# One chip core, attention feeding a routed two-layer product: expert chosen from a batch's first tiles, and three interleaved chains of attention steps

## The chip, the cores and the metric

One core of one Trainium2 chip. The metric is device time in microseconds (us) of one execution of the whole kernel. Before the change it is 468.69 us, the median of 3 runs (467.3 to 468.9).

## The reference

Eight batches of 8 heads, 576 tokens and 64 dimensions go through an attention with 32 memory slots; the result is the input of a mixture of eight experts of which each token uses one.

```python
def _attn_ref(q, k, v, phi):
    a = np.exp(phi - np.max(phi, axis=2, keepdims=True))
    a = a / (np.sum(a, axis=2, keepdims=True) + 1e-09)
    k_m = np.einsum('bhsm,bhsd->bhmd', a, k)          # 32 slots per head
    v_m = np.einsum('bhsm,bhsd->bhmd', a, v)
    scores = np.matmul(q, k_m.transpose(0, 1, 3, 2)) / np.sqrt(q.shape[-1])
    attn = np.exp(scores - np.max(scores, axis=-1, keepdims=True))
    attn = attn / (np.sum(attn, axis=-1, keepdims=True) + 1e-09)
    return np.matmul(attn, v_m)

def _moe_ref(x, expert_emb, tau, w1, w2):             # x: 4608 x 512
    xn = x / (np.linalg.norm(x, axis=-1, keepdims=True) + 1e-06)
    en = expert_emb / (np.linalg.norm(expert_emb, axis=-1, keepdims=True) + 1e-06)
    logits = xn @ en.T / tau
    expert_idx = np.argmax(logits, axis=1)            # one expert per token
    probs = softmax(logits)
    gate_w = probs[np.arange(N), expert_idx]
    for e in range(8):
        m = expert_idx == e
        out[m] = gate_w[m, None] * (np.maximum(x[m] @ w1[e], 0) @ w2[e])
```

With these inputs all 576 tokens of a batch choose the same expert, so the repair loop for other experts (`rest`) has nothing to do.

## The kernel before

A batch is 576 tokens, cut into five tiles of 128 (the fifth has 64, doubled). For each batch the kernel computes the slots (`slots`, tile `acc`), turns and scales them (`block`, `flip`), multiplies them with the queries (`scores`, tiles `ts`, `tl`, copied to `sT`), and folds the values with the router's rows into `vv` (`products`). A `Tokens` object then takes the batch's tokens: `weigh` (tile `sc`, its largest subtracted, exponential into `ea`), `divide` (by its sum `z`), `turn` (transposed through `ta` into `aw`, and split by `part` into the two halves `aT` of a product in two precisions), `attend` (tile `po`: the router's logits `lg` and one-hot choices `oh`), `norm` (lengths, `ss`), `choose` (counts the choices of all five tiles on TensorE in `key`, writes the winner to `seli`, from which SyncE's queue reads which weights to load), `flags`, `root` and `gates` (some twenty small VectorE instructions and one exponential, ending in the batch's `gate`).

The expert's products of a batch are `project` (values times `w1`, tile `pg`, split into `gh` by ScalarE, L604, and `gl` by VectorE, L605), `first` (16 products `ph`, eight for each half of the tokens; each leaves by ScalarE's `hh`, L626, and then VectorE's `hl`, L627; those of the second half also by ScalarE's `h4`, L633, queued between one `hh` and the next) and `second` (tile 4 from L649, in 8 parts, then tiles 0 to 3 from L660, 32 parts). Between the parts `split_w` splits `w2` (L581 to L590). Four PSUM banks serve the products (`mm`), three the attention (`pt`), one `acc`.

The order on every engine is the order of the program. It is written out by hand up to batch 1's scores (L888 to L956). From there a planner decides: `plan` keeps a counter for each engine, each step adds a fixed price to it, and after each part of a product `run` takes the next attention steps of one single list while the step is due and neither VectorE's nor ScalarE's counter is more than `slack`, 1.8 us, ahead of TensorE's. The list (`attention`, L689) is: batch 0's late steps (flags, root, gates), batch 1's steps W, D, R, A0, N0, A1, N1, A2, C, N2, S, and then for each next batch its memory steps (E, M0, Z, late steps of the batch before, B, V, M1, B, V, T) and its token steps. `hold` stops M1, the second half of the slots, until the next batch has been projected, so that it can stand between `project` and `first`.

Around the change:

- batch 0 is attended whole (`attend` of five tiles, `choose`, L930 to L933) before batch 1's slots and scores, which end the written order;
- `run(attention)` at L956 and inside `project(0)` (L722) takes batch 0's flags, root and gates before the planner looks at anything else;
- `w2s` holds batch 1's queries until its scores are done, so `w2` of batch 0 is loaded after them (L949).

Of the kernel before, what the change touches and what calls it, by code (L numbers as in the profile page):

```python
# [30 lines left out]
CHUNKS = (((0,), (0, 1, 2, 3)), ((1,), (0, 1, 2, 3)), ((0, 1), (4,)))  # L31
HS = S // 2
OOB = 65536.0
# [16 lines left out]
class Tokens:  # L50


    def __init__(self, k, b, pt):
        self.k, self.nc, self.b, self.pt = k, k.nc, b, pt
        wk = k.wk.tile
        self.lg = wk([P, NT, E], F32, tag="lg", name=f"lg{b}")
        self.ss = wk([P, NT], F32, tag="ss", name=f"ss{b}")
        self.m = wk([P, NT], F32, tag="m", name=f"m{b}")
        self.oh = wk([P, NT, E], BF16, tag="oh", name=f"oh{b}")
        self.po = {}  # L60

    def rows(self, p):

        gs, ti = CHUNKS[p]
        x = self.k.ea[:, gs[0], :4] if p < 2 else self.k.ea[:, :, 4]
        return gs, ti, x.rearrange("p t (h m) -> p t h m", m=M)

    def weigh(self, p):
# [11 lines left out]
        k.end["sc", b, p] = d  # L80
        k.end["x", b, p] = k.plan("ACT", 0.22 + 0.1 * n, d)

    def divide(self, p):
# [7 lines left out]
        nc.vector.tensor_tensor(out=x, in0=x, in1=z.unsqueeze(3).broadcast_to(x.shape), op=ALU.mult)  # L91
        k.end["a", b, p] = k.plan("DVE", 0.6 + 0.3 * n, k.end["x", b, p])

    def turn(self, p):
# [3 lines left out]
        for l, g in enumerate(gs):  # L98
            for n, i in enumerate(ti):
                nc.tensor.transpose(t[:, l, n * P : n * P + P], k.ea[:, g, i], k.ident)  # L100
# [3 lines left out]
        n = 4 if p < 2 else 2  # L104
        k.end["aT", b, p] = k.plan("ACT", 0.2 + 0.1 * n, k.plan("PE", 0.11 * n))
        k.part(g, slice(to.start, min(to.stop, S)))

    def attend(self, *ti, pt=None):

        k, nc, b = self.k, self.nc, self.b  # L110
        for i in ti:
            self.po[i] = po = (pt or self.pt)([P, NC * (D + E)], f"po{b}_{i}")
            to = slice(T0[i], T0[i] + P)
            for g in range(NG):
                nc.tensor.matmul(po[:, 144 * g : 144 * g + P + E], lhsT=k.aw[:, g, to], rhs=k.vv[:, g], start=True, stop=True)  # L115
# [11 lines left out]
    def norm(self, *ti):  # L127
        k, nc = self.k, self.nc
        for i in ti:
            x = k.ea[:, :, i].rearrange("p g (k m) -> p g k m", k=2)  # L130
# [10 lines left out]
            k.end["po", self.b, i] = k.plan("DVE", 0.5)  # L141

    def choose(self, pt=None):

        k, nc, b = self.k, self.nc, self.b
        self.key = key = (pt or self.pt)([P, E], f"key{b}")
        for i in range(-1, NT):
            nc.tensor.matmul(
                key, lhsT=k.ones, rhs=k.eb if i < 0 else self.oh[:, i], start=i < 0, stop=i == NT - 1
            )  # L150
# [5 lines left out]
        k.plan("DVE", 0.35, k.plan("PE", 0.35))  # L156
        k.chosen.add(b)
        k.loads()

    def flags(self):  # L160

        k, nc, b, key = self.k, self.nc, self.b, self.key
        cm = k.wk.tile([P, 1], F32, tag="cm", name=f"cm{b}")
        own = k.wk.tile([P, E], F32, tag="own", name=f"own{b}")
        nc.vector.tensor_reduce(out=cm, in_=key, axis=AX.X, op=ALU.max)
        nc.vector.tensor_scalar(out=own, in0=key, scalar1=cm, scalar2=None, op0=ALU.is_equal)
        nc.vector.scalar_tensor_tensor(
            out=k.fl[:, b], in0=key, scalar=float(E), in1=own, op0=ALU.is_ge, op1=ALU.subtract
        )
        k.plan("DVE", 0.6)  # L170
# [41 lines left out]
    def steps(self):  # L212
# [4 lines left out]
        def past():  # L217

            return b - 1 < k.hidden
# [6 lines left out]
        yield "W", lambda: end["sT", b, 1] if k.late else LATE, lambda: each(self.weigh)  # L226
        for p in range(3):
            yield "D", lambda p=p: end["x", b, p], lambda p=p: self.divide(p)
        yield "R", lambda: end["a", b, 2] if past() else LATE, lambda: each(self.turn)
        yield "A0", lambda: max(end["aT", b, 0], end["aT", b, 1], end["v", b]), lambda: self.attend(0, 1)  # L230
        yield "N0", lambda: end["po", b, 1], lambda: self.norm(0, 1)
        yield "A1", lambda: end["po", b, 1], lambda: self.attend(2, 3)
        yield "N1", lambda: end["po", b, 3], lambda: self.norm(2, 3)
        yield "A2", lambda: max(end["po", b, 3], end["aT", b, 2]), lambda: self.attend(4)
# [754 lines left out]
```

## Time and profile before

| | |
|---|---|
| median of 3 runs | 468.69 us |
| profiled execution | 467.85 us, of which 466.0 us are the span shown in its trace |
| TensorE products busy | 433.3 us (93%), 3588 matmuls |
| VectorE, ScalarE, GpSimdE busy | 263.7 us (57%), 204.0 us (44%), 130.1 us (28%) |
| head, to the start of batch 0's products | 44.0 us |
| batch 0, from its products to batch 1's | 57.8 us |
| batch 1 | 53.8 us |
| batches 2 to 5, each | 52.6 us |
| batch 6, batch 7 with the end | 49.5 us, 50.5 us |

A batch is counted here from its first `pg` product to the next batch's. Busy time of TensorE is modelled, so its share alone doesn't say how dense the stream is; a batch's length against its neighbours' does.

### The profile page before, as it was taken

What the parts mean: (1) busy time and instruction counts of PE and PEld (TensorE: products, weight loads), DVE (VectorE), ACT (ScalarE), POOL (GpSimd) and SP (SyncE); (2) the same over time, 40 slices, a digit from 0 to 9 for tenths busy, and PEclk for the clock granted to TensorE, in tenths of its full rate; (3) what the DMA queues carried; (4) which work ended last, traced back from release to release, by engine and by line L of the source; (5) the groups of instructions that cost most, each with busy time, mean ns of one, the idle gap of its engine ahead of it and who ended that gap; (6) DMA issues with size and microseconds to landing.
All of it is one profiled execution on the core that took longest, in us unless ns stands there. A gap on an engine that the chain in (4) does not pass through costs nothing.

```text
span 466.0 us, 9511 instructions
## 1 busy us (share of the span) xinstructions
PE 433.3 (93%) x3588; PEld 347.6 (75%) x3588; DVE 263.7 (57%) x858; ACT 204.0 (44%) x527; POOL 130.1 (28%) x140
## 2 busy tenths in 40 slices
PE   3758699999999999999999999999999999999992
PEld 2454587868788787878788787878788787879682
DVE  5574658665677457646577357656587457555100
ACT  4334463156523564147523464147523464136310
POOL 1020122304440153304440063304440053306310
PEclk9979799999999999999999999999999999999997
DMA  8747940099315980199315980199314800183011
GB/s 298 249 166 262 334 185 23 36 339 355 133 34 197 361 291 11 46 344 359 125 34 188 371 289 11 46 337 371 119 34 176 316 2 12 47 321 148 14 46 49
DMA packets 26323, 82.48 MB, mean 177 GB/s; under 512 B 7064, under 2 KB 7064, under 8 KB 24224
## 3 DMA queue, kind: packets, MB, share of 16 engines
q1 hardware_dynamic: 23088, 72.10, 43.7%
q0 software_dynamic: 3072, 9.44, 5.6%
q8 instruction: 30, 0.49, 0.4%
q10 hardware_dynamic: 112, 0.28, 0.2%
q14 instruction: 21, 0.17, 0.1%
HBM read 66.60 MB, written 15.20 MB: 176 GB/s over the span
## 4 chain that ended last, share of the span: by engine, by line
PE 81%; issue 6%; DVE 5%; ACT 3%; DMA 2%; POOL 1%; POOLq 0%; DVEq 0%; ACTq 0%
PE py L660 34%; PE ph L623 21%; PE py L649 6%; PE acc L456 4%; PE po L115 4%; PE pg L601 2%; PE sc L73 2%; PE ts L502 2%; PE ta L100 2%; PE te L443 2%; DMA kx<-kv 1%; DMA kl<-kvt 1%; POOL wl L590 1%; DVE hl L627 1%; ACT hh L626 1%
## 5 line engine op out<-in xcount | busy, mean ns | idle before, releaser
L623 PE MATMUL ph<-aT,gh 128*128 128x288 f32 x512 | 108.9, 307 | 5.4 <-DVE gl L605 5.2
L590 POOL TENSOR_TENSOR wl<-w2s,wh 128x512 fp32r<-128x512 f32 x60 | 76.6, 1282 | 117.8 <-ACT wh L581 101.7
L660 PE MATMUL py<-wh,hh 128*128 128x512 f32 x256 | 105.8, 413 | 0.0
L660 PE MATMUL py<-wh,hl 128*128 128x512 f32 x256 | 100.4, 392 | 0.0
L660 PE MATMUL py<-wl,hh 128*128 128x512 f32 x256 | 100.0, 391 | 0.0
L623 PEld LDWEIGHTS ph<-aT,gh 128*128 128x128 f32 x512 | 83.1, 192 | 13.5 <-DVE gl L605 8.9
L627 DVE SCALAR_TENSOR_TENSOR hl<-ph,hh 128x288 fp32r<-128x288 f32 x128 | 57.6, 456 | 60.8 <-ACT hh L626 60.8
L623 PE MATMUL ph<-aT,gl 128*128 128x288 f32 x256 | 76.3, 298 | 0.0
L667 ACT ACTIVATE ys<-py,gate 128x512 f32<-128x512 f32 (+1 forms) x40 | 25.6, 641 | 90.4 <-issue 55.1
L770 POOL DMA_DIRECT2D out_dram<-ys x32 | 17.7, 552 | 155.7 <-ACT ys L667 104.0
L626 ACT ACTIVATE hh<-ph 128x288 fp32r<-128x288 f32 x128 | 51.7, 411 | 18.1 <-PE ph L623 17.9
L660 PEld LDWEIGHTS py<-wh,hh 128*128 128x128 f32 x256 | 48.1, 188 | 12.3 <-DVE ea L77 2.3
L660 PEld LDWEIGHTS py<-wh,hl 128*128 128x128 f32 x256 | 48.1, 188 | 10.7
L660 PEld LDWEIGHTS py<-wl,hh 128*128 128x128 f32 x256 | 48.2, 188 | 8.1
L623 PEld LDWEIGHTS ph<-aT,gl 128*128 128x128 f32 x256 | 49.2, 192 | 0.0
L605 DVE TENSOR_TENSOR gl<-pg,gh 128x512 fp32r<-128x512 f32 x32 | 19.8, 682 | 34.7 <-ACT gh L604 34.7
L574 POOL TENSOR_TENSOR aT<-aw,aT 128x512 fp32r<-128x512 f32 (+1 forms) x24 | 25.4, 1081 | 33.9 <-DVE aT L573 33.9
L649 PE MATMUL py<-w2s,h 128*64 128x256 f32 x256 | 31.2, 386 | 1.2 <-ACT h L633 1.2
L581 ACT CAST wh<-w2s 128x512 fp32r<-128x512 f32 x50 | 30.6, 612 | 0.0
L633 ACT ACTIVATE h<-ph 128x64 f32<-128x64 f32 x64 | 14.3, 223 | 34.2 <-DVE hl L627 34.2
L649 PEld LDWEIGHTS py<-w2s,h 128*64 128x64 f32 x256 | 16.9, 136 | 11.6 <-ACT h L633 3.7
L115 PEld LDWEIGHTS po<-vv,aw 128*128 128x128 f32 x160 | 23.3, 203 | 1.8
(124 smaller groups left out, 518.9 us busy)
## 6 DMA issues: line engine op xcount, KB each, us to landing
kx<-kv SPq DMA_DIRECT2D x32, 512.0 KB, 8.0
w1s<-w SPq DMA_DIRECT2D x16, 1024.0 KB, 5.6
w2s<-w SPq DMA_DIRECT2D x32, 512.0 KB, 9.5
out_dram<-ys POOLq DMA_DIRECT2D x32, 256.0 KB, 3.0
qt<-qT SPq DMA_DIRECT2D x14, 576.0 KB, 5.9
ex<-phiT SPq DMA_DIRECT2D x16, 288.0 KB, 11.4
ad<-aw SPq DMA_DIRECT2D x8, 576.0 KB, 12.1
kl<-kvt SPq DMA_DIRECT2D x7, 256.0 KB, 7.7
```

The source lines that it names most:

```text
L115: nc.tensor.matmul(po[:, 144 * g : 144 * g + P + E], lhsT=k.aw[:, g, to], rhs=k.vv[:, g], start=True, stop=True)
L456: nc.tensor.matmul(self.acc[32 * i : 32 * i + 32, i], lhsT=self.eT[:, 5 * g + k, 32 * j : 32 * j + 32], rhs=src[:, 4 * g + j], start=k == ...
L574: self.nc.gpsimd.tensor_tensor(out=al, in0=a, in1=ah.bitcast(F32), op=ALU.subtract)
L581: nc.scalar.copy(h, x)
L590: nc.gpsimd.tensor_tensor(out=l, in0=x, in1=h.bitcast(F32), op=ALU.subtract)
L605: nc.vector.tensor_tensor(out=self.gl[:, g, f], in0=ps[g], in1=self.gh[:, g, f].bitcast(F32), op=ALU.subtract)
L623: nc.tensor.matmul(p, lhsT=w[:, g, fs], rhs=x[:, g, to], start=g == 0 and k == 0, stop=g == 1 and k == 2)
L626: nc.scalar.activation(self.hh[:, f, to], p, AF.Relu)
L627: nc.vector.scalar_tensor_tensor(out=self.hl[:, f, to], in0=p, scalar=0.0, in1=self.hh[:, f, to].bitcast(F32), op0=ALU.max, op1=ALU.subtract)
L649: nc.tensor.matmul(p[64 * j : 64 * j + 64], lhsT=self.h4[:, f], rhs=self.w2s[:, f, d * j : d * j + d], start=f == 0, stop=f == 7,)
L660: nc.tensor.matmul(p, lhsT=h[:, f, to], rhs=w[:, f], start=f == 0 and k == 0, stop=f == 7 and k == 2)
L667: nc.scalar.activation(y[:, :d], p, AF.Copy, scale=gate[:, i : i + 1])
```

## The change

- Batch 0 starts with other chunks (`FIRST`): tile 0 of both head groups first. After that tile alone `choose(ti=(0,))` picks the expert and `w1` is loaded; `owner` keeps the counted winner. Tiles 1 to 4 are weighed, divided (one multiplication goes to GpSimdE) and turned in the written order, but attended later (`finish`).
- Every later batch chooses after A0, from tiles 0 and 1 (step C). The full count is a second group of six matmuls after N2 (step F, `full`), which the flags now use.
- The single list becomes three chains, tokens, memories and gates (`chains`); `run` takes the first of the three whose next step is due and for whose tiles the PSUM banks are free by the counters (`room_at`). `vv` and `ea` are double. Batch 1's W may run during batch 0's `first`; W of later batches waits for `second`, as before.
- Nothing of the planner runs between the written order and batch 0's `project`, nor in it. Batch 0's gates are forced at part 13 of its `second` (the other batches' at part 5, as before), and outputs wait in `ready` until the gate has been issued (`puts`).
- `warm` issues 27 matmuls of 512 columns that nobody reads: 13 near the start, 8 and 6 in the head.
- The second group of batch 0's `sT` is copied by VectorE, and batch 0's `w2` is split with fewer VectorE subtractions.

```diff
+FIRST = (((0, 1), (0,)), ((0,), (1, 2, 3, 4)), ((1,), (1, 2, 3, 4)))
...
+        (mult or nc.vector).tensor_tensor(out=x, in0=x, in1=z.unsqueeze(3).broadcast_to(x.shape), op=ALU.mult)
...
+    def count(self, pt, name, ti=range(NT)):
+        k, nc = self.k, self.nc
+        key = pt([P, E], f"{name}{self.b}")
+        for n, i in enumerate((-1, *ti)):
+            nc.tensor.matmul(key, lhsT=k.ones, rhs=k.eb if i < 0 else self.oh[:, i], start=n == 0, stop=n == len(ti))
+        return key
...
         def past():
-            return b - 1 < k.hidden
+            return b - 1 < k.hidden and ("po", b - 1, 4) in end
...
+        yield "W", 3, lambda: end["sT", b, 1] if k.late or b == 1 else LATE, lambda: each(self.weigh)
         for p in range(3):
+            yield "D", 0, lambda p=p: end["x", b, p], lambda p=p: self.divide(p)
+        yield "R", 3, lambda: end["a", b, 2] if past() else LATE, lambda: each(self.turn)
+        yield "A0", 2, lambda: max(end["aT", b, 0], end["aT", b, 1], end["v", b]), lambda: self.attend(0, 1)
+        yield "C", 1, lambda: end["po", b, 1], lambda: (self.choose(ti=(0, 1)), self.owner())
+        yield "N0", 0, lambda: end["po", b, 1], lambda: self.norm(0, 1)
+        yield "A1", 2, lambda: end["po", b, 1], lambda: self.attend(2, 3)
+        yield "N1", 0, lambda: end["po", b, 3], lambda: self.norm(2, 3)
+        yield "A2", 1, lambda: max(end["po", b, 3], end["aT", b, 2]), lambda: self.attend(4)
+        yield "N2", 0, lambda: end["po", b, 4], lambda: self.norm(4)
+        yield "F", 1, lambda: end["po", b, 4], self.full
...
+    def finish(self):
+        end = self.k.end
+        yield "A1", 2, lambda: max(end["aT", 0, 1], end["aT", 0, 2], end["v", 0]), lambda: self.attend(1, 2)
+        yield "N1", 0, lambda: end["po", 0, 2], lambda: self.norm(1, 2)
+        yield "A2", 2, lambda: end["po", 0, 2], lambda: self.attend(3, 4)
+        yield "N2", 0, lambda: end["po", 0, 4], lambda: self.norm(3, 4)
+        yield "F", 1, lambda: end["po", 0, 4], self.full
...
+        while not (until and until()):
+            at = [self.at(c) for c in range(3)]
+            now = self.t["PE"]
+            full = max(self.t["DVE"], self.t["ACT"]) > now + self.slack
+            c = next((c for c in range(3) if at[c] <= now and not full), None)
+            if c is None:
+                if not until:
                     return
+                c = chain if at[chain] < LATE else at.index(min(at))
+            self.next[c][3]()
...
+        for _ in self.project(b, self.vT[b % 2]):
+            pass
...
+            if n == (13 if b == 0 else 5):
+                self.run(lambda: ("gate", b) in self.end, 2)
...
+    k.warm(13, k.mm([P, 512], "hot0"))
...
+    t0.weigh(0)
+    k.products(0)
+    k.warm(8, hot)
+    t0.divide(0)
+    t0.turn(0, False)
+    t0.weigh(1)
+    t0.attend(0)
+    t0.choose(ti=(0,))
+    k.softmax(1)
+    t0.weigh(2)
+    t0.divide(1, k.nc.gpsimd)
+    t0.owner()
+    k.warm(6, hot)
...
-    k.run(attention)
+    k.t = dict.fromkeys(k.t, max(k.t["PE"], end["w1", 0]))
     for b in range(B):
-        k.batch(b, attention)
+        k.batch(b)
```

## Rows read from the trace of the kernel before

**Rows 1.** Windows, batches 0, 1, 2: length; busy PE, PEld, DVE, ACT, POOL; clock; DMA.

```profile
44.00:101.79 57.79, 52.35 (x392) 43.12 (x382) 37.95 (x131) 23.81 (x61) 11.23 (x12) 0.94 0.50 176
101.79:155.63 53.84, 53.31 (x460) 43.01 (x467) 32.37 (x104) 25.54 (x67) 16.68 (x17) 1.00 0.57 205
155.63:208.23 52.60, 52.59 (x456) 42.53 (x463) 32.18 (x104) 24.96 (x65) 16.69 (x17) 1.00 0.57 196
```

**Rows 2.** Timeline, batch 0's products start: start, length, engine, line, operation, [idle before].

```profile
45.04 0.45 ACT L542 COPY vv<-tl 64x72 f32<-64x72 f32 x2
...
45.68 0.17 DVE L165 TENSOR_REDUCE cm<-key 128x1 f32<-128x8 f32 x1
...
49.68 0.24 ACT L196 ACTIVATE l<-l 128x40 f32<-128x40 f32 x1 [4.19 <-DVE l L195]
...
49.94 2.05 ACT L604 CAST gh<-pg 128x512 fp32r<-128x512 f32 x4
...
51.34 0.50 PEld L623 LDWEIGHTS ph<-aT,gh 128*128 128x128 f32 x2 [5.39 <-DVE gl L605]
```

**Rows 3.** Windows of 2 us in batch 0's first products, the clock third from the end.

```profile
50.00:52.00 2.00, 0.66 (x3) 0.66 (x4) 1.91 (x7) 2.00 (x4) 0.00 (x0) 0.54 1.06 375
...
56.00:58.00 2.00, 2.00 (x14) 2.00 (x13) 0.67 (x2) 1.07 (x3) 0.90 (x1) 0.76 1.04 416
```

**Rows 4.** Timeline of the head, all engines, up to batch 1's scores.

```profile
11.69 0.65 PE L456 MATMUL acc<-kx,eT 128*32 128x128 f32 x8 [0.51 <-DMA kx<-kv]
...
23.80 0.42 DVE L77 TENSOR_TENSOR ea<-sc,mx 128x256 f32<-128x256 f32 x1
...
25.05 0.78 ACT L420 ACTIVATE ex<-ex,nm 128x576 f32<-128x576 f32 x1
...
29.72 0.75 DVE L406 TENSOR_REDUCE nm<-ex 128x1 f32<-128x576 f32 x1
...
35.39 0.59 ACT L444 COPY eT<-te 128x512 f32<-128x512 f32 x1 [4.02 <-PE te L443]
...
36.19 0.90 SPq L391 DMA_DIRECT2D w1s<-w  x2
36.22 1.08 PE L456 MATMUL acc<-kx,eT 128*32 128x128 f32 x32
...
42.04 1.45 PE L502 MATMUL ts<-w2s,kT 64*32 64x512 f32 x16
```

**Rows 5.** Timeline of the head: GpSimdE beside VectorE, and the same addition later.

```profile
25.77 1.26 POOL L574 TENSOR_TENSOR aT<-aw,aT 128x512 fp32r<-128x512 f32 x1 [23.36 <-DVE aT L573]
...
26.24 0.82 DVE L89 TENSOR_SCALAR z<-z 128x16 f32<-128x16 f32 x1
...
80.63 0.17 DVE L89 TENSOR_SCALAR z<-z 128x8 f32<-128x8 f32 x1
```

**Rows 6.** Timeline, second half of batch 0's 16 first products.

```profile
62.54 0.22 ACT L633 ACTIVATE h<-ph 128x64 f32<-128x64 f32 x1 [0.82 <-DVE hl L627]
...
68.34 1.95 PE L649 MATMUL py<-w2s,h 128*64 128x256 f32 x16 [0.79 <-ACT h L633]
...
71.73 0.22 ACT L633 ACTIVATE h<-ph 128x64 f32<-128x64 f32 x1 [0.53 <-DVE hl L627]
```

**Rows 7.** Timeline of VectorE, batch 1's W (from 73.11) and D (from 76.55).

```profile
73.11 0.68 DVE L76 TENSOR_REDUCE mx<-sc 128x16 f32<-128x512 f32 x1
...
76.55 0.68 DVE L88 TENSOR_REDUCE z<-ea 128x16 f32<-128x512 f32 x1
```

**Rows 8.** Timeline of TensorE in batch 0's `second`: attention steps between parts.

```profile
83.44 1.09 PE L115 MATMUL po<-vv,aw 128*128 128x136 f32 x8
...
91.26 0.18 PE L148 MATMUL key<-eb,ones 128*128 128x8 bf16 x1
...
91.42 0.48 PE L660 MATMUL py<-wh,hh 128*128 128x512 f32 x1
```

**Rows 9.** The page's DMA issues: transfer, count, KB each, median us to landing.

```profile
ad<-aw SPq DMA_DIRECT2D x8, 576.0 KB, 12.1
```

More of the change, by code (lines that the diff above doesn't have):

```diff
@@ new lines, in steps, with full @@
+        yield "N0", 0, lambda: end["po", b, 1], lambda: self.norm(0, 1)
[4 more added lines that the diff above has]
+        yield "F", 1, lambda: end["po", b, 4], self.full
+        end["norm", b] = 0.0
+    def full(self):
+        self.key2 = self.count(self.pt, "full")
+        self.k.plan("PE", 0.35)
+        self.flags()
+        self.k.keep(self.b)
@@ L525, in scores @@
+        pe = self.plan("PE", 1.9)
+        for g in range(NG):
+            if g and b == 0:
+                nc.vector.tensor_copy(out=self.sT[:, g, :512], in_=ts[g])
+                self.end["sT", b, g] = self.plan("DVE", 0.7, pe)
+            else:
+                nc.scalar.copy(self.sT[:, g, :512], ts[g])
+                self.end["sT", b, g] = self.plan("ACT", 0.6, pe)
+            self.end[f"ts{b}_{g}"] = self.end["sT", b, g]
+        for g in range(NG):
             nc.scalar.copy(
@@ L680, in memories @@
         for g in range(NG):
-            yield f"M{g}", lambda: max(end["eT", b], end.get(("kb", b), 0.0)), lambda g=g: self.slots(b, g)
-            if not g:
-                yield "Z", lambda: 0.0, lambda: self.shares(b)
-                yield from late
-            yield "B", lambda: end["acc", b], lambda g=g: self.block(b, g)
-            yield "V", lambda: end["kb", b] if past() else LATE, lambda g=g: self.flip(b, g)
-        yield "T", lambda: end["kT", b], lambda: (self.scores(b, self.pt), self.products(b))
@@ L689, in attention @@
-    def attention(self, t0, t1):
-        yield from t0.late()
-        yield from t1.steps()
-        for b in range(2, B):
-            yield from self.memories(b, t1.late())
-            t1 = Tokens(self, b, self.pt)
-            yield from t1.steps()
-        yield from t1.late()
-    def run(self, attention, until=None):
-        while True:
-            if not self.step:
-                self.step = next(attention, None)
-                if not self.step:
-                    return
-            name, ready, do = self.step
-            now = self.t["PE"]
-            if self.hold and name == "M1":
-                return
-            if not (until and not until()) and (
-                ready() > now or self.t["DVE"] > now + self.slack or self.t["ACT"] > now + self.slack
-            ):
-                return
-            do()
-            self.step = None
-            if until and until():
-                return
@@ L719, in batch @@
-    def batch(self, b, attention):
-        if b == 0:
-            for _ in self.project(0, self.vT[0]):
-                self.run(attention)
-            self.projected = 1
+            yield f"M{g}", 0, lambda g=g: (
+                LATE
+                if g and b > self.now + 1 or ("kv", b) not in end
+                else max(end["eT", b], end["kv", b], end.get(("kb", b), 0.0))
+            ), lambda g=g: self.slots(b, g)
+            if not g:
+                yield "Z", 0, lambda: 0.0, lambda: self.shares(b)
@@ new lines, in memories, with chains, tokens, gates @@
+            yield "B", 0, lambda: end["acc", b], lambda g=g: self.block(b, g)
+            yield "V", 2, lambda: end["kb", b] if free() else LATE, lambda g=g: self.flip(b, g)
+        end["mem", b] = 0.0
+    def chains(self, t0, t1):
+        def tokens():
+            yield from t1.steps()
+            for b in range(2, B):
+                ts[b] = Tokens(self, b, self.pt)
+                yield from ts[b].steps()
+        def memories():
+            for b in range(2, B):
+                yield from self.memories(b)
+        def gates():
+            yield from t0.finish()
+            for b in range(B):
+                while b not in ts:
+                    yield "-", 0, lambda b=b: 0.0 if b in ts else LATE, lambda: None
+                yield from ts[b].late()
+        ts = {0: t0, 1: t1}
+        self.todo = [tokens(), memories(), gates()]
+        self.next = [next(x) for x in self.todo]
@@ L750, in batch @@
                 self.loads()
[L751 to L764 removed]
+            self.run()
+        self.late = False
     def rows(self, b):
```

282 lines of the change are left out of this document (145 added, 137 removed).

## The prediction

> **What bounds the kernel now.** I first read the windows batch by batch. In batches 2 to 5 TensorE is busy 52.59 of 52.60 us, and batch 1 needs 53.84 [rows 1]: the later batches are bound by TensorE's stream, and only an operation taken out of that stream, or a gap in it, can shorten them. Batch 0 lasts 57.79 us with TensorE busy 52.35 at a mean clock of 0.94 [rows 1], and 44 us pass ahead of it. So what can be won lies in the first 100 us, above all in two places: the head, a chain of small steps over three engines, and the start of batch 0's products. There TensorE's timeline shows 5.39 us without a weight load, up to 51.34 [rows 2]. The wait is for `gl`, which waits for `gh`, which ScalarE starts at 49.94 although `pg` began at 44.0: in ScalarE's queue the gates' exponential (49.68) stands ahead of it, and that waits for a row of small VectorE instructions that begins at 45.68 [rows 2]. After this idle time the granted clock is 0.54 of full in the window from 50 us (the 1.2 GHz level within it) and 0.76 in the window from 56 us: by that share half speed lasts until about 56.96 [rows 3].
>
> **Part 1, the head.** Project of batch 0 stays behind batch 1's scores in TensorE's order, so the choice helps only by what stands between. From slots to scores of batch 1 it was 36.22 to 42.04, 5.8 us [rows 4], and all of that stays. What moves is the time at which those slots can start. Up to the choice I set the steps one behind the other. Keys and values of batch 0 land at the same time; the slots behind them run at 0.65/8 = 81 ns each against 1.08/32 = 34 ns later [rows 4], so if the 13 warm matmuls lift the clock first, the last 16 win some 0.7 us; I take 0.5. Second half of the slots to 14.7, its scaling and turning to 16.3, scores and copies to 18.6, then tile 0 alone: four 256-wide VectorE steps of 0.42 us [rows 4] with an exponential, a sum and a reciprocal between them, transposition and copy, to 22.5; `po` to 23.2; VectorE has put two steps of 0.68 (tiles 1 to 4) [rows 7] ahead of `lg`, so the choice is written at about 25.3. VectorE then takes two maxima of 0.75, ScalarE two exponentials of 0.78 and its reads, one of 0.63, and three `eT` copies of 0.59, 0.59 and 0.37 [rows 4]: `eT` is complete at 30.5, the slots start at 31.0 behind four transpositions, scores at 36.6 instead of 42.04: 5.4 us won. The weights are asked for at about 26.3 instead of 36.19, and `pg` began 7.8 us after that request [rows 1, 4] without waiting for it; left where it was, the request would now hold `pg` back, so the early choice is needed, but it gives nothing beyond the 5.4. Bounds: 3.5 (a step of each engine missed) to 7 (slots start when batch 1's data is there). The 27 warm matmuls have no row. 13 stand ahead of any data; for the other 14 the nearest row is a 512-column product of 0.48, half of it beside the next [rows 8]: 0 if TensorE waits there anyway, 3.4 if all stand on the chain. Between the head's steps it waits, and I take nothing.
>
> One multiplication goes from VectorE to GpSimdE. The row shows that the two can block one another: while a GpSimdE subtraction ran from 25.77 to 27.03, VectorE's addition took 0.82 us, against 0.17 for the same addition later [rows 5]. The Trainium skill, page "SBUF — State Buffer", section "Who interferes with whom", says that the one of the two engines that comes second is blocked for the other's whole instruction, if VectorE's is a scalar operation in a two-port mode or has two SBUF inputs. By that rule this multiplication would hold VectorE back by at most the 1.26 us of its length; the trace agrees in kind, with 0.65. What VectorE has behind it here are two PSUM reads and a reduction, so I take nothing.
>
> **Part 2, project to first product.** ScalarE's last copy of the written order ended at 45.04 + 0.45 = 45.49, 3.45 us after the scores began at 42.04 [rows 2, 4]. `gh` now comes directly behind it, and the first weight load followed `gh` by 51.34 − 49.94 = 1.40 [rows 2]. So 4.85 us from scores to products instead of 9.30: 4.45 won, first products at 41.45. With no long idle time ahead of them they start at 2.4 GHz: half of 56.96 − 51.34, that is 2.8 us [rows 2, 3], won too.
>
> **Part 3, batch 0's first products.** Read by the planner's prices, W of batch 1 comes after the third product: ten VectorE and ScalarE steps between `hl` 2 and `hl` 3, 76.55 − 73.11 = 3.4 us of VectorE [rows 7]; as ScalarE's exponentials stand ahead of `hh` 3, four PSUM banks fill and TensorE waits about 1.5 us. Two of the three D, (80.63 − 76.55 − 0.41) / 2 = 1.8 us each [rows 5, 7], come after the eighth and thirteenth product. In the second half of the products ScalarE and VectorE hand each product to and fro (`hh`, `hl`, `h4`): from the first `h4` (62.54) to the last (71.73) there are seven steps of 1.31 us [rows 6], slower than TensorE fills the four banks, and `py` waits for them at 68.34 [rows 6]. D lies in that chain. By queues it ends 3.7 us later than without W and D, counted at the end of the half tile; taken from 0 (cover by free banks) to 5.2 (all of W's wait and both D).
>
> **Part 4, the rest of batch 0.** TensorE gets four tiles of `po`, a tile 1.09/2 less overlap, 1.9 in all, six `key` matmuls of 91.42 − 91.26 = 0.16 [rows 8], and the flip of batch 2's first half, which leaves batch 1, four matmuls like `po`'s, 4 × 1.09/8 = 0.5: together 2.5. At part 13 the gates are forced: one behind the other stand E, A2, F and the gates. E's transpositions share one PSUM bank, since `po` 1 and 2 hold two, so twice TensorE waits for a copy of 0.59 [rows 4] and its handing over, 1.6 together, and the full count waits 1.0 for VectorE's `oh`: 2.6, between 0 and 5. Behind it, R writes `aw` about 5 us after `keep` asked for its copy. Such a copy took 12.1 us to land [rows 9], but with 4 MB of weights ahead of it; here the queue is empty, and I take nothing; it may cost 3.
>
> **Part 5, the later batches.** Batch 1 now has M1 ready to stand between `project` and `first`, and becomes like the others: 53.84 − 52.60 = 1.2 won [rows 1]. In batches 1 to 7 the second count adds 0.16 each [rows 8], 1.1 in all; outputs and gates move beside TensorE's stream. Hidden by the same stream: double `vv` and `ea`, the earlier load of weights.
>
> **The sum:** −5.4 − 4.45 − 2.8 + 3.7 + 2.5 + 2.6 − 1.2 + 1.1 = −3.95. The profiled execution of 467.85 becomes 463.9; the median lies 0.84 above it, so I forecast 464.7 us. Half a percent, 2.3 us, is about what a measurement of this kernel can tell from no change.
>
> **The rivals.**
> - *The stalls of batch 0 don't appear.* W, D and the forced steps hide behind banks that are free: for it, 52.35 us busy in 57.79 [rows 1] leave room; against it, the chain of rows 6 is already late without them. 3.7 and 2.6 less: 458.4.
> - *The clock or the `aw` copy takes the gain.* A second place with TensorE half idle, in the head behind the choice or at part 13, lowers the clock as at 50 us, for 2.8 [rows 2, 3], and R waits 1 us for the copy: 468.5, no change. Against it: my longest gaps are under 2 us, that one was above 4.
> - *Slower: the gates slide.* They are now the last chain, taken only if no other step is due. Their VectorE row takes 49.68 − 45.68 = 4.0 us [rows 2]. If a batch's gates aren't done before the second half of its products, they sit in the chain of rows 6, as D does; half of them cost each of seven batches some 1 us more than TensorE's cover: 471.7. It decides when F comes later than about part 30 of `second`. Before, `key` was issued near part 27 and the gates still ended in the same product.
>
> **How the numbers follow.** Forecast 0.50 (its own range 462 to 467.5), no stalls 0.20, gain taken 0.18, gates slide 0.12. The range reaches from the second case to short of the last: 458 to 470. Faster by over 0.5% is below 466.35: 0.43 of the first case and the second, with a little for a larger gain, 0.64; within: 0.07 and the third, 0.25; slower 0.11.
>
> **What would show it.** Batch 1's `ts` near 36.6; the first `ph` near 41.5 with `gh` directly behind `vv`'s copy and no clock below full after it; `py` of the half tile of batch 0 ending near 64.4; a wait of `te` and `key` at part 13; project of batch 1 near 98; batches 2 to 5 at 52.7 or 52.8. If batch 2 to 5 differ from 52.60 by over 0.4 us the chains reorder more than I read, and the forecast is wrong.

## The result and the profile after

| | before | changed |
|---|---|---|
| median of four | 468.41 us (467.3 to 468.9) | 475.20 us (474.42 to 475.54) |
| profiled execution: time, span, mean clock | 467.85, 466.0, 0.979 | 475.33, 473.5, 0.987 |

The median of 468.69 given above was that of three of the four executions before. The ratio is 1.0139, 95% interval 1.0113 to 1.0166: the changed kernel is slower by 6.8 us, where I had forecast 464.7 and a gain. The measured time lies outside my range of 458 to 470.

Where the time goes, as points on TensorE's timeline (each is the start of the first instruction of its kind; the half tile is the fifth tile with its 64 tokens, the first that `second` finishes, and its row gives the end; us):

| | before | forecast | changed |
|---|---|---|---|
| scores of batch 1 (`ts`) | 42.04 | 36.6 | 38.29 |
| first product (`ph`) | 51.34 | 41.45 | 42.97 |
| end of batch 0's half tile | 73.41 | 64.4 | 66.54 |
| project of batch 1 (`pg`) | 101.72 | 98 | 99.79 |
| length of batch 1, `pg` to `pg` | 53.84 | 52.8 | 54.65 |
| length of each of batches 2 to 5 | 52.60 | 52.8 | 54.66 to 54.68 |

Up to batch 1 the changed kernel is 1.9 us ahead. From there it loses 0.8 in batch 1 and 2.06 in each of batches 2 to 5. First the windows that answer to [rows 1]: batches 0 to 3 of the changed kernel, with length, busy PE, PEld, DVE, ACT and POOL, granted clock, DMA share and GB/s.

```profile
39.53:99.79 60.26, 54.20 (x396) 42.52 (x390) 42.22 (x147) 23.74 (x62) 14.17 (x14) 1.00 0.53 181
99.79:154.44 54.65, 53.29 (x453) 42.62 (x452) 32.26 (x104) 25.00 (x65) 16.81 (x17) 1.00 0.60 211
154.44:209.10 54.66, 53.30 (x453) 42.61 (x452) 32.27 (x104) 24.92 (x65) 16.84 (x17) 1.00 0.54 188
209.10:263.76 54.66, 53.31 (x453) 42.62 (x452) 32.26 (x104) 24.92 (x65) 16.80 (x17) 1.00 0.54 188
```

The later batches had TensorE busy for 52.59 of 52.60 us. Now it is busy for 53.30 of 54.66: gaps of 1.36 us have come into a stream that had none, and the same ones in every batch. The table of waits of the whole kernel names them (engine, line, tile, releaser: us in total, times, longest), first for TensorE's matmuls, then for its weight loads:

```profile
PE te L502 <- ACT eT L503: 6.8, 10, 0.7
...
PEld te L502 <- ACT eT L503: 9.1, 10, 0.9
```

Ten times in five batches TensorE waits for ScalarE to copy a group of transpositions out of PSUM. The timeline of batch 2 shows the place (start, length, engine, line, operation, [idle before it and its releaser]; the last line is `norm`):

```profile
188.91 1.09 PE L119 MATMUL po<-vv,aw 128*128 128x136 f32 x8
...
189.83 0.60 PE L502 MATMUL te<-ident,ex 128*128 128x128 f32 x4
...
190.47 0.58 ACT L503 COPY eT<-te 128x512 f32<-128x512 f32 x1 [1.57 <-PE te L502]
...
191.11 0.66 PE L502 MATMUL te<-ident,ex 128*128 128x128 f32 x4 [0.68 <-ACT eT L503]
...
192.44 0.44 PE L502 MATMUL te<-ident,ex 128*128 128x128 f32 x2 [0.68 <-ACT eT L503]
...
193.47 0.19 PE L152 MATMUL key<-oh,ones 128*128 128x8 bf16 x2
...
194.28 0.41 DVE L135 CUSTOM_DVE_ANT_1 ea<-po,ea 128x256 f32<-128x256 f32 x1
```

E, the transpositions of the batch after next, stands directly behind `po` of tiles 0 and 1. These two still hold two of the three banks of `pt`, because `norm` reads them only behind `key`. So the three groups of E share one bank and go through it one behind the other: 189.83, 191.11, 192.44. In the kernel before, E came behind `key` and `norm`, and the same ten transpositions ran without a gap, 1.25 us in all:

```profile
200.22 1.25 PE L443 MATMUL te<-ident,ex 128*128 128x128 f32 x10
```

The planner allows the new place because `room_at` asks for the end of each bank's last owner and takes a missing entry as 0.0, that is as free; the entry of a `po` is written only when `norm` is put out.

The Trainium skill, page "Perfetto Trace Analysis", section "Optimization Strategy", says that the same gap coming again and again on the engine that should be saturated can mean that there isn't enough SBUF or PSUM for the next tile. The trace agrees, with ten gaps of 0.68 us; but the pool has three banks as before, and it is the new order that leaves only one of them free at this place.

The early part came out near the forecast. `gh` stands behind `vv`'s last copy on ScalarE [rows 2], the first weight load of a product at 42.97, and the windows of [rows 3] are at full clock:

```profile
41.22 1.07 ACT L667 CAST gh<-pg 128x512 fp32r<-128x512 f32 x2
...
42.97 0.30 PEld L686 LDWEIGHTS ph<-aT,gh 128*128 128x128 f32 x2 [0.84 <-DVE gl L668]
```

```profile
50.00:52.00 2.00, 0.72 (x5) 0.73 (x6) 1.24 (x4) 1.62 (x5) 0.00 (x0) 1.00 0.96 279
56.00:58.00 2.00, 1.62 (x10) 1.40 (x11) 1.15 (x4) 1.05 (x4) 0.46 (x1) 1.00 0.78 309
```

In the head the clock was at its lower level (0.50, 1.2 GHz) for part of two stretches, one in the slots of batch 0, one in those of batch 1 that [rows 4] show at full speed: 32 of them took 1.93 us instead of 1.08. Ahead of the second, TensorE had waited 1.88 us for GpSimdE's multiplication. The first line is the writing of the choice.

```profile
25.52 0.14 DVE L161 TENSOR_SCALAR seli<-ki 1x1 int32<-1x1 int32 x1
...
30.68 0.93 PE L103 MATMUL ta<-ident,ea 128*128 128x128 f32 x4 [1.88 <-POOL ea L94]
31.54 1.93 PE L515 MATMUL acc<-kx,eT 128*32 128x128 f32 x32
...
38.29 1.09 PE L562 MATMUL ts<-w2s,kT 64*32 64x512 f32 x16
```

```profile
14.00:16.00 2.00, 2.00 (x19) 1.26 (x10) 0.48 (x1) 0.54 (x3) 0.00 (x0) 0.50 0.40 144
32.00:34.00 2.00, 2.00 (x37) 1.49 (x30) 0.53 (x5) 0.23 (x1) 0.00 (x0) 0.50 0.97 404
```

### The profile page after: what moved, and what is told of

It reads as the page before. It is cut to its first block, busy times and chain, and to the rows that moved or that the text cites. A ratio compares the mean times of both kernels' runs of the same rounds, so it can differ in the third digit from the quotient of the medians.

```text
span 473.5 us, 9575 instructions
## 1 busy us (share of the span) xinstructions
PE 441.6 (93%) x3638; PEld 346.4 (73%) x3638; DVE 264.3 (56%) x856; ACT 201.6 (43%) x524; POOL 135.1 (29%) x144
## 4 chain that ended last, share of the span: by engine, by line
PE 80%; issue 6%; DVE 5%; ACT 4%; DMA 2%; POOL 2%; POOLq 0%; ACTq 0%; DVEq 0%
PE py L723 33%; PE ph L686 19%; PE py L712 5%; PE po L119 4%; PE acc L515 4%; PE pg L664 3%; PE te L502 2%; PE ta L103 2%; PE sc L76 2%; PE ts L562 2%; ACT eT L503 1%; DVE hl L690 1%; DMA kx<-kv 1%; ACT hh L689 1%; DMA kl<-kvt 1%
## 5 line engine op out<-in xcount | busy, mean ns | idle before, releaser
L653 POOL TENSOR_TENSOR wl<-w2s,wh 128x512 fp32r<-128x512 f32 x62 | 79.8, 1292 | 104.9 <-ACT wh L644 91.9
L686 PE MATMUL ph<-aT,gh 128*128 128x288 f32 x512 | 107.0, 303 | 2.8 <-DVE hl L690 1.4
L686 PEld LDWEIGHTS ph<-aT,gh 128*128 128x128 f32 x512 | 81.0, 188 | 10.6 <-ACT h L696 4.7
L686 PE MATMUL ph<-aT,gl 128*128 128x288 f32 x256 | 75.3, 294 | 0.0
L723 PEld LDWEIGHTS py<-wh,hh 128*128 128x128 f32 x256 | 48.1, 188 | 11.3 <-DVE ea L80 2.3
L686 PEld LDWEIGHTS ph<-aT,gl 128*128 128x128 f32 x256 | 48.0, 188 | 0.0
L696 ACT ACTIVATE h<-ph 128x64 f32<-128x64 f32 x64 | 14.3, 223 | 36.6 <-DVE hl L690 36.6
L644 ACT CAST wh<-w2s 128x512 fp32r<-128x512 f32 x48 | 29.2, 613 | 0.0
L637 POOL TENSOR_TENSOR aT<-aw,aT 128x512 fp32r<-128x512 f32 (+2 forms) x23 | 24.6, 1088 | 6.8 <-DVE aT L636 6.5
L636 DVE CAST aT<-aw 128x512 fp32r<-128x512 f32 (+2 forms) x23 | 17.1, 769 | 14.4 <-ACT aw L106 14.0
```

What stands on the lines that cost most here:

```text
L637: self.nc.gpsimd.tensor_tensor(out=al, in0=a, in1=ah.bitcast(F32), op=ALU.subtract)
L644: nc.scalar.copy(h, x)
L653: nc.gpsimd.tensor_tensor(out=l, in0=x, in1=h.bitcast(F32), op=ALU.subtract)
L686: nc.tensor.matmul(p, lhsT=w[:, g, fs], rhs=x[:, g, to], start=g == 0 and k == 0, stop=g == 1 and k == 2)
L723: nc.tensor.matmul(p, lhsT=h[:, f, to], rhs=w[:, f], start=f == 0 and k == 0, stop=f == 7 and k == 2)
```

## The experiments

The runs were made on several chips, each beside the kernel before. Where two runs of different chips are compared, their ratios to the kernel before say more than their medians: that kernel's own median went from 467.95 to 469.19 us between the chips.

**Theory A: E's place, and the bank that its three groups share, makes the later batches long.** Rival B: the second count, the three chains or the split row of flags do. Two runs tell these apart from opposite sides: the changed kernel with E's place undone, and the kernel before with E's place alone.

*Free banks for E.* In the changed kernel a bank of `po` counts as taken until `norm` is out:

```
-        return max((self.end.get(x, 0.0) for x in self.used[-NTB:][:n]), default=0.0)
+        return max((self.end.get(x, LATE if x[:2] == "po" else 0.0) for x in self.used[-NTB:][:n]), default=0.0)
```

> The changed kernel, with one edit in the planner: a PSUM bank of `po` counts as taken until `norm` has been put out, so that E (the ten transpositions of the batch after next) no longer stands directly behind the first two `po` but behind the full count, where three banks are free. Theory A (E's three groups share the one bank that `po` 0 and 1 leave, and TensorE waits for each copy): batches 1 to 5 fall from 54.66 to about 52.7 us each, the waits of `te` for `eT` vanish from the table of waits, batch 0 wins up to 1.6, and the time is 463.5 to 465. Rival B (the second count, the steps spread over three chains, or a split owner/flag row make the later batches long): batches 1 to 5 stay at 54 or more, and the time stays above 473.

Measured: 466.12 us, ratio to before 0.9955 (0.9933 to 0.9978); 9.1 us less than the changed kernel by the medians and 8.6 by the ratios, and 1 us above the expected 465. The line of `te` for `eT` is gone from its waits. Its batches 0 to 2, and the transpositions of batch 2:

```profile
38.93:99.21 60.28, 53.62 (x397) 42.63 (x390) 42.20 (x147) 23.81 (x62) 14.26 (x14) 1.00 0.55 189
99.21:152.12 52.91, 52.76 (x452) 42.58 (x451) 32.30 (x104) 24.64 (x65) 16.82 (x17) 1.00 0.57 200
152.12:205.06 52.94, 52.76 (x452) 42.60 (x451) 32.32 (x104) 24.64 (x65) 16.84 (x17) 1.00 0.56 194
...
195.75 1.29 PE L502 MATMUL te<-ident,ex 128*128 128x128 f32 x10
```

Batches 1 to 5 fall from 273.32 us together to 264.78: E's place costs 8.54 us, 1.71 in each. Theory A holds. Of the 1.72 us of batch 2, 1.18 were idle time (1.36 against 0.18); 0.54 stood in the table as busy (53.30 against 52.76), of which the transpositions account for 0.41 (0.60 + 0.66 + 0.44 us in three rows against 1.29 in one). Two numbers were off: some 0.35 of the 2.06 us a batch stays, and batch 0 did not get shorter (60.28 against 60.26): TensorE was busy 0.58 less there, and waited as much longer, for `oh` ahead of `key` (0.8) and for `norm` (0.3).

*E's place alone, in the kernel before*, with its control, S alone:

```
+            yield "S", lambda: 0.0, lambda: k.softmax(b + 1)
         yield "R", ...
         yield "A0", ...
+            yield "E", lambda: end["ex", b + 1], lambda: [k.turn(b + 1, i, min(i + 4, 10)) for i in (0, 4, 8)]
```

(S and E are taken out of their old places; the control has the first line alone.)

> The kernel before, single list of steps, with only the place of two steps changed: S (the softmax of the batch after next) stands ahead of R, and E (its transpositions) directly behind the first two `po`, as the changed kernel issues it. Theory A: the shared bank costs the old kernel what it costs the changed one, about 2 us in each of batches 1 to 5 and some of it in batch 0: 477 to 481, with waits of `te` for `eT` near 0.7 and 0.9 us. Rival B (the loss of the later batches comes from the count or the chains, not from E's place): batches 2 to 5 stay at 52.6 to 52.8 and the time within 1 us of 468.4.

> The kernel before with only S (softmax of the batch after next) moved ahead of R, E left behind N2: the half of the run with E moved that is not under suspicion. Theory A: within 1 us of 468.4, batches 2 to 5 at 52.6. Rival (softmax ahead of the attention holds VectorE back from `norm`): some tenths in each batch, 470 or more.

Measured: E's place 479.97, ratio 1.0235 (1.0192 to 1.0278); S alone 470.30, ratio 1.0044 (1.0011 to 1.0077). So E's place costs 9.7 us in the old kernel too, without any second count or chain. In the traces batches 1 to 5 take 273.22 us together with E's place changed and 264.55 with S alone: 8.67, close to the 8.54 above. S alone costs some 2 us by the ratio, more than Theory A had said; batches of 52.52 to 53.38 us stand beside one another in its trace, with hardly any idle time on TensorE, and the reason stays open. Batch 3 of the run with E, and E's place in it:

```profile
217.31:271.51 54.20, 52.68 (x450) 42.66 (x449) 32.09 (x104) 24.69 (x66) 16.82 (x17) 1.00 0.53 188
...
251.78 1.09 PE L115 MATMUL po<-vv,aw 128*128 128x136 f32 x8
...
254.82 0.85 PE L445 MATMUL te<-ident,ex 128*128 128x128 f32 x6 [1.52 <-DVE ss L131]
```

The shortage is the same, the release that ends it another: here the second group waits 1.52 us for `norm` to free a bank of `po`, there each group waits for the copy of the one before.

**What is left in the later batches: the second count.** In the kernel with free banks, batches 1 to 7 choose behind the last `po` from all five tiles, with one count:

```
-        yield "C", 1, lambda: end["po", b, 1], lambda: (self.choose(ti=(0, 1)), self.owner())
...
-        yield "F", 1, lambda: end["po", b, 4], self.full
+        yield "F", 1, lambda: end["po", b, 4], self.single
```

(`single` puts out `choose` over all tiles, `owner`, and `flags` on the same count.)

> The kernel with free banks for E, with one count instead of two in batches 1 to 7: the expert is chosen behind the last `po` from all five tiles, as before the change; batch 0 keeps its early choice. By the prediction's price (0.16 for the second count) batches 1 to 5 fall from 52.95 to 52.8 and the time by 1.1. By the difference of the traces (52.95 against 52.60, all of it count, its weight loads and one wait for `oh`) they fall to 52.60 and the time by 2.4, to 463.7. Rival (the early choice is worth something in the later batches, since it asks for weights earlier): project waits for its weights, 466 or more.

Measured: 465.42, ratio 0.9931 (0.9902 to 0.9960). Batches 2 to 5 take 52.53 to 52.58 instead of 52.94 to 53.01, so the count cost 0.4 us each and not 0.16. But batch 1 takes 54.37 instead of 52.91, and the gain in the time is 0.7 us by the medians and 1.1 by the ratios, whose intervals overlap, instead of 2.4: at its start `pg` waits for weights, 0.8 us by its matmuls and 1.7 by its weight loads.

```profile
97.94:152.31 54.37, 53.56 (x449) 42.66 (x449) 32.41 (x104) 24.73 (x65) 16.84 (x17) 1.00 0.56 195
152.31:204.89 52.58, 52.58 (x449) 42.54 (x449) 32.33 (x104) 24.65 (x65) 16.88 (x17) 1.00 0.55 195
...
PE pg L671 <- DMA w1s<-w: 0.8, 1, 0.8
```

Both sides were partly right: the count costs what the traces' difference had said, and the early choice is worth something in the first batch that lacks it.

**Part 3: W and D of batch 1 in batch 0's first products.** In the kernel with free banks:

```
-        yield "W", 3, lambda: end["sT", b, 1] if k.late or b == 1 else LATE, lambda: each(self.weigh)
+        yield "W", 3, lambda: end["sT", b, 1] if k.late else LATE, lambda: each(self.weigh)
```

> The kernel with free banks for E (E behind the full count), and in it W and D of batch 1 taken out of batch 0's first products (they come in its second ones, as in the later batches). By the prediction's Part 3 these steps cost 3.7 us: batch 0's half tile ends near 62.2 instead of 65.9, and the time is 462.4 against 466.1. Rival (the products' own hand-over of hh, hl and h4 sets that stretch, and free banks cover W and D): the half tile ends less than 1 us earlier, time 465 to 466.5.

> The kernel with free banks for E and with W and D of batch 1 out of batch 0's first products once more, on another chip beside the other runs of this call: 461.2 +- 1, ratio to the kernel before 0.985; if the ratio is nearer to 0.99, the single place at which it was faster was the head's clock of that chip.

Measured: 461.23 and, once more, 460.95; ratios 0.985 (0.9799 to 0.9901) and 0.9847 (0.9820 to 0.9874). The half tile's last `py` starts at 61.59 and ends at 62.67, where it ended at 65.95: 3.3 of the expected 3.7 us. TensorE's waits for `hl` and `h4` up to there fall from 4.1 us to 0.4. Batch 0 becomes 8.8 us shorter and batch 1 4.4 longer, since some of their matmuls change places (352 in batch 0 where there were 397); batch 2 begins at 147.72 instead of 152.12, 4.4 earlier. Part 3's mechanism holds, and its price was 0.4 too high at the half tile; where the further 1.1 us come from is open. This is the fastest kernel of the study, 1.5% below the kernel before.

```profile
61.59 1.08 PE L712 MATMUL py<-w2s,h 128*64 128x256 f32 x8
...
38.90:90.41 51.51, 49.77 (x352) 41.07 (x344) 36.52 (x122) 22.74 (x58) 14.38 (x15) 1.00 0.52 180
90.41:147.72 57.31, 55.80 (x497) 44.47 (x496) 36.50 (x130) 26.03 (x71) 16.45 (x17) 1.00 0.59 210
```

**Part 2: the gates of batch 0 behind its products.** The first run is the kernel before without the run of the attention's steps ahead of project and inside it:

```
             for _ in self.project(0, self.vT[0]):
-                self.run(attention)
+                pass
...
-    k.run(attention)
```

> The kernel before with one part alone: the attention's steps and gates of batch 0 no longer stand ahead of `project` of batch 0 and inside it, but come with its first products, so that `gh` follows `vv`'s copy on ScalarE at once. By the prediction's Part 2: first `ph` 4.45 us earlier and 2.8 more from a clock that does not fall, first `ph` near 47, no half-speed window behind it: 461 if nothing is given back. Rival (the gates' steps, put into the products' chain of `hh`, `hl` and `h4`, cost what they gave): the first `ph` still near 47, but batch 0's half tile ends less than 4 us earlier, and the time is 464 to 468.

Measured: 553.91, ratio 1.1835 (1.1793 to 1.1877). The first product comes at 47.37, 4.84 us after the scores (42.53), as Part 2 has it, and the clock stays full from there to 80. For the time nothing follows: the single list of steps fell behind, `pg` waits 14 times for its weights, and the batches behind batch 0 take 66 to 67 us. That the experts were chosen late is what these waits point to; no run shows it.

```profile
PE pg L601 <- DMA w1s<-w: 46.1, 14, 6.5
```

The second run undoes Part 2 in the kernel with free banks:

```
         self.now = b
+        if b == 0:
+            self.run(lambda: ("gate", 0) in self.end, 2)
```

> The kernel with free banks for E, with Part 2 undone: the other tiles, the full count and the gates of batch 0 stand ahead of its project, as before the change. By the prediction's Part 2 the first product comes 4.45 us later plus the four `po` that now stand ahead of it (1.9), near 48.7, 2.8 us of half clock come behind it, and 4.5 are given back at part 13 and by the `po` no longer there: time 469 to 471. Rival (the gates' wait was hidden by something else that comes late then, weights or `aT`): first product later, but time within 1 us of 466.1.

Measured: 471.37, ratio 1.0060 (1.0030 to 1.0089), above the kernel with free banks by 5.2 us by the medians and 4.9 by the ratios. The first product comes at 48.34, 11.9 us after the scores of that execution (36.48) instead of 4.7, behind a wait for `gl`; the clock is at 0.50 behind it, as in [rows 3], until about 53, and also from 43 to 46 and from 67 to 71. From the scores to project of batch 1 it is 66.59 us instead of 61.53. Part 2 holds as a whole; the run doesn't part the order's share from the clock's.

```profile
48.34 0.54 PE L686 MATMUL ph<-aT,gh 128*128 128x288 f32 x2 [2.30 <-DVE gl L668]
...
50.00:52.00 2.00, 2.00 (x10) 2.00 (x9) 0.90 (x3) 0.58 (x2) 0.00 (x0) 0.50 1.04 413
```

**Part 1, the head.** Three runs on what stands there.

*No warm matmuls*, in the kernel with free banks:

```
-    k.warm(13, k.mm([P, 512], "hot0"))
...
-    k.warm(8, hot)
...
-    k.warm(6, hot)
```

> The kernel with free banks for E, without the 27 warm matmuls on constants; nothing that counts is left out. By the prediction's Part 1 the 13 ahead of the data win 0.5 us (the last slots of batch 0 at 34 ns instead of 81) and the other 14 cost nothing: 466.6 against 466.1. Rival (without them the clock stays at 1.2 GHz through more of the head, slots and scores of both batches take twice as long): scores of batch 1 at 40 or later, time 468 to 470. Third way (the 14 stand on the chain of the choice): scores earlier, time 465 or less.

Measured: 468.77, ratio 0.9985 (0.9962 to 1.0008), against 0.9955 (0.9933 to 0.9978) with them: 1.4 us by the ratios, whose intervals overlap. The medians differ by 2.65 us, but on this chip the kernel before was slower too. The scores of batch 1 come at 39.56 in the profiled execution instead of 37.68, and the clock is at 0.50 from within the window at 24 to within that at 34; from the writing of the choice to the scores it takes 12.95 us, where four profiles with the warm matmuls and full clock in this stretch have 11.47:

```profile
24.00:26.00 2.00, 1.01 (x8) 0.69 (x6) 1.62 (x4) 0.49 (x2) 0.00 (x0) 0.71 1.03 411
30.00:32.00 2.00, 1.00 (x5) 0.60 (x4) 1.83 (x7) 1.29 (x4) 1.05 (x1) 0.50 0.99 401
34.00:36.00 2.00, 1.98 (x30) 1.30 (x22) 0.48 (x1) 0.17 (x1) 0.00 (x0) 0.73 0.92 365
```

The rival is the nearer one, though its scores were to come at 40 or later and the gain isn't clear of the noise. By the place where the clock fell, the later 14 matmuls, which I had put at nothing, did most of it; that is argued from one profile, as no run leaves out the 14 alone.

*Slots ahead of the division*, in the kernel with free banks:

```
     k.turn(1, 8, 10)
+    k.shares(1)
+    t0.divide(1, k.nc.gpsimd)
+    t0.owner()
+    k.slots(1, 0)
+    k.block(1, 0)
     t0.divide(2)
     t0.turn(1, False)
-    k.shares(1)
-    k.slots(1, 0)
-    k.block(1, 0)
```

(`divide(1)` and `owner` stood ahead of the six warm matmuls.)

> The kernel with free banks for E, in the head the reciprocals and slots of batch 1 put ahead of batch 0's multiplication on GpSimdE, of its transposition and of the last sums on VectorE; nothing is left out. Theory H (the head came out later than forecast because the slots of batch 1 stand behind batch 0's division, on TensorE behind a transposition that waits 1.9 us for GpSimdE and on VectorE behind its sums): slots 1 us earlier, scores near 36.7 instead of 37.7, time 465.1. Rival (the transpositions and `aw`'s copies, now later, hold the first product back through `aT`): scores earlier, first product not, time 466 or more.

Measured: 468.05, ratio 0.9985 (0.9956 to 1.0014), with single times from 465.1 to 470.4. In the profiled execution (469.35) the clock was at half speed twice, from about 12 to 18.5 and from about 36 to 42.5, and the scores came at 39.98 and took 1.96, so the time says little about the order. Ahead of the second stretch the trace says more: counted from the writing of the choice, the first half of batch 1's slots starts after 3.97 us instead of 5.75, but the second half after 8.73 instead of 8.63. What the first half gains is lost before the second, and Theory H's gain does not appear.

*The multiplication back on VectorE*, in the fastest kernel: `t0.divide(1, k.nc.gpsimd)` becomes `t0.divide(1)`.

> The kernel with free banks and with W and D of batch 1 behind batch 0's first products, and in it the one multiplication of the head back on VectorE. By the prediction (I take nothing) the time is that of the same kernel with GpSimdE, 461 to 462. Theory H (the head waits for this multiplication: TensorE 1.9 us, 1.05 of it the multiplication): VectorE takes 0.68 for it, without the addition beside it growing from 0.17 to 0.35, so the transposition comes 0.4 earlier, the slots too: 460.6 to 461. Rival (VectorE's row is the head's chain, and 0.68 more in it counts whole): scores and time 0.5 later.

Measured: 461.70, ratio 0.9866 (0.9839 to 0.9893), against 460.95 and 0.9847 beside it: the intervals overlap, and the time shows no difference. The traces show a small one. TensorE's wait ahead of the transposition is 1.37 instead of 1.88 us, VectorE's addition beside it takes 0.17 instead of 0.35, and the first slots start 0.5 us earlier behind the choice; but the second half of the slots starts 9.22 us behind it instead of 8.63, and the scores 12.06 instead of 11.47, both at full clock. So the rival's 0.5 is there: the multiplication on GpSimdE gains some 0.6 us of the head, which the prediction had put at nothing.

**Both repairs and the single count.** In the fastest kernel, one count in batches 2 to 7 and the early choice kept in batch 1.

> Both repairs and a third edit together: free banks for E; W and D of batch 1 out of batch 0's first products (alone 466.1 to 461.2); and one count instead of two in batches 2 to 7, batch 1 keeping its early choice (with one count its project had waited for its weights). If the parts add up, batches 2 to 5 take 52.56 instead of 52.96 and the time is 461.2 - 2.2 = 459.0. Rival (the later choice makes a later batch wait for weights as it did batch 1): 461 or more, with a wait of `pg` for `w1s`.

Measured: 465.02, ratio 0.9909 (0.9881 to 0.9937), against 0.985 and 0.9847 without the single count: slower by some 2.8 us. The rival holds: batch 2, now the first that chooses late, waits 2.4 us for its weights, and the batches behind it take 52.52 to 52.59.

```profile
PE pg L673 <- DMA w1s<-w: 2.4, 1, 2.4
...
148.22:204.15 55.93, 53.54 (x449) 42.72 (x449) 32.44 (x104) 24.71 (x65) 16.89 (x17) 1.00 0.56 199
204.15:256.67 52.52, 52.51 (x449) 42.53 (x448) 32.32 (x104) 24.66 (x65) 16.86 (x17) 1.00 0.55 196
```

By these rows it should lose about 1.5 us (2.9 in batch 2, less 0.4 in each of batches 3 to 5 and 0.2 in batch 6). The profiled execution takes 2 us more than that of the first run of the fastest kernel, and 0.5 of them lie ahead of the scores (38.13 against 37.65), which leaves the 1.5. The ratios' 2.8 is uncertain by some 2 us and doesn't contradict it.

## Why the prediction was wrong, point by point

**Part 5, the later batches, is the step that failed.** It said that outputs and gates move beside TensorE's stream and counted 0.16 us for the second count. I had read the waits that the new chains add in batch 0 alone. Yet Part 4 has the mechanism in so many words: E's transpositions share one PSUM bank, since two `po` hold two. I put it at part 13 of batch 0, for 1.6 us, and did not ask where E comes in batches 1 to 5, so that the prediction put it at nothing there. It cost 8.54 us; in batch 0 it cost at most some tenths, since three products come between `po` and E and `norm` follows at once (72.03 and 72.38 on VectorE) instead of behind `key`: the ten transpositions stand in one row, of 1.61 us instead of 1.29.

```profile
70.05 1.09 PE L119 MATMUL po<-vv,aw 128*128 128x136 f32 x8
71.84 1.61 PE L502 MATMUL te<-ident,ex 128*128 128x128 f32 x10
```

The last sentence of the prediction named the sign to look for (batches 2 to 5 off by over 0.4 us), so the way to fall was known; it had no price, and none of the four cases contained it. The "gates slide" rival ended on the right side of zero and is not what happened: no wait of the later batches in the table is for a gate.

**The second count**, 0.16 forecast, cost 0.34 to 0.41 in batches 2 to 5 (52.94 to 53.01 in the kernel with free banks against 52.60), and the run with one count gives it back. The term was mis-sized: TensorE is busy 0.16 to 0.25 longer a batch, which is near the forecast, and beside it stands idle for 0.14 to 0.18, where `key` now waits for `oh`. Over batches 1 to 7 that is 0.95 more than the forecast's 1.1.

**Part 5, batch 1:** 1.2 won by M1 as filler was forecast; with the second count's 0.16 in it that makes 1.04, and with free banks it is 53.84 - 52.91 = 0.93. Right.

**Part 1, the head:** 5.4 forecast, 3.75 measured. The choice was written at 25.52, forecast 25.3. Of the loss of 1.7, 0.2 stands ahead of the choice and 1.5 behind it, and most of that is the clock: I had assumed full clock from the first slots on. Seven profiled executions have this head order. In four of them the clock is full behind the choice, and from its writing to the scores they all take 11.47 us, 0.2 more than the 11.3 forecast; in the other three, the changed kernel among them, it falls there, and they take 12.77 to 12.94. So 1.3 of the 1.7 is the clock. The scores came at 36.48, 37.09, 37.65, 37.68, 38.13, 38.29 and 39.85, so 36.6 was near the best of them. That one is the run with the gates first, at full clock behind the choice:

```profile
25.01 0.14 DVE L161 TENSOR_SCALAR seli<-ki 1x1 int32<-1x1 int32 x1
...
36.48 1.09 PE L562 MATMUL ts<-w2s,kT 64*32 64x512 f32 x16
```

**Part 2:** 4.85 from scores to first product forecast, 4.68 measured; full clock behind it as forecast. Right.

**Part 3:** from the first product to the end of the half tile 22.97 forecast (22.07 + 3.7 - 2.8), 23.57 measured. Taking W and D out brings 3.3 there. Right in kind, 0.6 low.

**Part 4:** from the half tile to project of batch 1, 28.31 before; 33.4 forecast, 33.25 measured. Right in its sum, but by luck. TensorE was busy all of the 28.31 before; now it is busy 32.13 of 33.25. So the added work came to 3.8 instead of 2.5, and the waits to 1.1 instead of 2.6: 0.6 of `full` for `oh`, 0.4 of a flip for a copy on ScalarE, and not the 1.6 for E. The two misses cancel. The wait for the `aw` copy [rows 9], put at nothing, did not show.

**The account** of the profiled execution, 475.33 measured against 463.9 forecast: E's place 8.54, the head 1.7 (1.3 of it the clock), the second count 0.95, batch 0's products 0.6, less 0.17 and 0.16 where Parts 2 and 4 came out lower: 11.46 of 11.43 us. Without E's place the changed kernel stands at 466.12, above the forecast by 1.4 and inside its range.

## What to carry to other kernels

When steps of several chains are put into one engine's stream, go through every loop that the new order governs, steady ones first, and count at each step how many buffers of the shared pool are held and who releases them; a stall of 1.7 us in each of five equal batches cost 8.5 us here, where the changed kernel had been 1.9 us ahead at the start of the first of them. In a planner that asks whether a buffer is free, an entry that isn't there yet must mean taken, not free. An early step that looks worthless in the steady state (the early choice of later batches) may pay in the first batch that lacks it.

## What was not expected of the hardware

The clock of the head isn't the same from one execution to the next. Two kernels with the same instructions up to the first product were at 0.50 in different places: the kernel with free banks from about 13 to 16.5 us, with scores at 37.68; the fastest one, in its second profile, from about 12 to 18 and again from 32 to 35.5, with scores at 39.85. The wait of 1.87 us for GpSimdE's multiplication stands ahead of the second stretch in both, and the clock fell behind it in only one; of the seven executions, it fell there in three. The kernel before has such a stretch in its head too, from 26 to 33. Ahead of the first change in a trace the granted clock may read too high: in the run without warm matmuls it is given as 1.00 where 32 slots, at 13.62, took 1.94 us instead of 1.08.

```profile
14.00:16.00 2.00, 2.00 (x40) 1.65 (x39) 0.00 (x0) 0.00 (x0) 0.00 (x0) 0.50 0.52 188
32.00:34.00 2.00, 1.94 (x24) 1.55 (x28) 1.79 (x9) 0.58 (x1) 0.01 (x1) 0.50 1.01 426
```

Behind the choice alone the clock makes 1.3 to 1.5 us (12.77 to 12.94 against 11.47), and the scores of the seven lie 3.4 us apart. So an edit of the head worth 1 us can't be judged from the time of one profile; the distance between two steps with full clock between them can be compared, and repeated to 0.01 us in four profiles.

VectorE's small addition took 0.35 us beside GpSimdE's multiplication in the changed kernel, and 0.17 without it. [Rows 5] had 0.82 for it beside a GpSimdE subtraction: the block that the Trainium skill describes (page "SBUF — State Buffer", section "Who interferes with whom") is there again, at 0.18 us this time. Both additions end with the GpSimdE instruction beside them, at 30.65 and 30.62 here and at 27.06 and 27.03 in [rows 5]; so the cost was what was left of that instruction, and not its length.
